# Five head pairs with some copies on other engines: ScalarE for VectorE, GpSimd for ScalarE

## The chip, the cores and the metric

The kernel runs on one core of a Trainium2 chip. A core has a matrix engine (TensorE, PE in the profile; its weight loads are PEld), and VectorE (DVE), ScalarE (ACT), GpSimd (POOL) and SyncE (SP), each with its own instruction queue, worked off in order. They meet through semaphores. SBUF is the on-chip memory, PSUM the eight banks that TensorE writes into; GpSimd works on SBUF here. The metric is the device time of one execution in microseconds: 692.33 us for the kernel before, the median of 3 runs (691.79 to 692.9). Lower is better.

## The reference

Attention with a threshold, for 8 batches of 8 heads, 576 positions, 64 columns per head, followed by a mixer:

```python
scores = scale * np.matmul(q, k.transpose(0, 1, 3, 2))
thresh = np.max(scores, axis=-1, keepdims=True) - tau
scores = np.where(scores >= thresh, scores, -1000000000.0)
scores = scores - np.max(scores, axis=-1, keepdims=True)
attn = np.exp(scores)
attn = attn / (np.sum(attn, axis=-1, keepdims=True) + 1e-09)
x = attn @ v                     # heads side by side: 576 x 512 per batch
h = x.transpose(0, 2, 1) @ U @ V # rank 32, along the positions
u = x + h.transpose(0, 2, 1)
out = u + np.maximum(u @ w_ch1, 0.0) @ w_ch2   # 512 -> 2048 -> 512
```

Inputs and output are float32. q, k and the scores are float32 in the kernel too; the weights of the attention, the turned u and the mixer are bf16, and v is split into two bf16 parts.

## The kernel before

**Tiling.** Two heads of a batch make a pair; there are 32 pairs, four to a batch. The 576 rows of a head are cut into four tiles of 128 and one of 64; the half tiles of two neighbouring pairs are put together, so an even pair has five row tiles (0 to 4) and an odd pair four (0 to 3). A row tile of two heads is a score step; there are 144 steps and 288 score tiles of 128 x 576.

**A step.** TensorE computes the scores (line 696) into one of two groups of three PSUM banks (`trio`). VectorE scales them into SBUF (`s_sb`) and keeps each row's least value `m` (line 725). GpSimd makes the threshold `thr` from `m` (line 742), a 128 x 2 instruction. ScalarE takes the exponential into `e_sb` (line 748). VectorE selects: it compares `s_sb` with `thr`, multiplies with `e_sb`, and sums each row (line 755), into `w_ring`. GpSimd doubles the last 64 columns (the twin copy, line 766), so that five blocks of 128 can be turned by TensorE into a PSUM bank (line 773). The turned weights are then copied from that bank into SBUF, `wT_ring` or `wT4`, by one 128 x 640 bf16 copy (line 781): head 0's by ScalarE, head 1's by VectorE, as the tuple `COPIED` says.

**The end of a pair.** TensorE multiplies the turned weights with the two parts of v (AV, lines 835 to 843). In the first four pairs ScalarE then takes the product to `x` (line 870) and GpSimd divides it by the row sums (line 874); later pairs do this through lines 890, 894 and 901. `narrow` makes a bf16 copy of x, `xb`, with two instructions on ScalarE (lines 906 and 907). TensorE applies U (914), ScalarE takes the result over as `tt` (920), TensorE applies V (929), VectorE adds it to x (936), which makes u. `narrow_u` makes the bf16 copy of u, `ub`, on ScalarE (943). TensorE turns it (951), ScalarE copies it out as `uT` (959).

**The mixer.** When the four pairs of a batch are done, its first product runs on TensorE in 16 pieces (line 1024, with 1040 for the half tile), ScalarE applies the ReLU (1014), and the second product (1057) gives the output tiles. These matmuls are spread among the score steps of later batches. W1 and W2 are loaded by GpSimd's queue in 8 pieces each (1127, 1130); q and k of the first pairs are loaded by SyncE, and of later pairs by GpSimd (563). v is loaded by SyncE (587).

**The order.** All work is written as tasks with an engine, a cost and what they depend on. A search, made beforehand, put the tasks in one order with those costs; its result is in the file as a list of task numbers, `ORDER`, and a table of the PSUM bank of each task, `BANK`. Negative numbers in the list are filler matmuls (line 526), whose result nobody uses. The kernel emits the tasks in the list's order, so each engine's queue is the list restricted to that engine. The costs stand in the code but nothing in the running kernel reads them.

Of the kernel before, what the change touches and what calls it, by code (L numbers as in the profile page):

```python
# [87 lines left out]
COPIED = (SCA, VEC)  # L88
PHASES = (1, 2, 3, 4, 5, 6, 8, 28)
# [4 lines left out]
HIGH = 32  # L94
# [20 lines left out]
class Task:  # L115
# [17 lines left out]
    24, 21, 26, 25, 19, 22, 23, 20, 1, 47, 0, 27, 45, 28, 44, 41, -1, -1, -1, -1, -1, -1, 32, 2, 34, 30, 46, 33, 35,  # L133
    31, 29, 48, -2, -2, 59, 43, 49, 61, 42, 60, 68, 39, -3, -3, -3, -3, -3, 73, 63, 62, 3, 69, 40, 74, 228, 70, 36,
    -8, -8, -8, 71, 75, 225, 77, 87, 64, 224, 56, 82, 72, 226, 89, 37, 227, -6, 52, 76, 88, 57, 50, 53, 231, 78,
    101, 4, 96, 83, 51, 90, 54, 102, 84, 55, 248, 65, 91, 38, 103, -8, -8, 85, 244, 115, 86, 110, 104, 92, 233, 79,
    105, 246, 117, 93, 58, 229, -3, -3, 94, 116, 80, 66, 249, 97, 81, 235, 130, 230, 67, 106, 95, 251, 111, 188,
    124, 247, 132, 112, 236, 118, 232, 98, 131, 107, 119, 245, -7, 108, 125, 189, 113, 99, 252, 109, 144, 120, 139,
    234, 100, 121, 250, 237, 126, 114, 5, 145, 122, 238, 191, 133, 146, 134, 140, 127, 153, 147, 239, 158, 128, 397,
    123, 141, 135, 192, 194, 240, 160, 148, 136, 142, 159, 241, 213, 149, 172, 214, 6, 195, 154, 167, 259, 150, 143,  # L140
    137, 161, 260, 257, 242, 174, 186, 138, 155, 243, 173, 258, -8, 156, 255, 162, 187, 157, 264, 175, 523, 181,
    168, 521, 256, 163, 169, 526, 266, 190, 151, 393, 265, 193, 152, 527, 196, 279, 7, 197, -7, -7, -7, -7, 207,
    402, 182, 164, 273, 524, 278, 267, 198, 176, 183, 396, 165, 274, 184, 166, 170, 129, 185, 275, 199, 280, 268,
    171, 399, -5, -5, 276, 177, 286, 291, 253, 269, 281, 178, 394, 277, 208, 8, 254, 282, 270, 179, 395, 205, 292,
    283, 200, 180, 525, 206, 293, 398, 210, 287, 300, 294, 400, 201, 288, 284, 392, 211, 261, 305, 289, 202, 271,
    306, 295, 262, 290, 272, 307, 296, 308, 318, 301, 313, 309, 285, 302, 319, 203, 297, 212, 405, 320, 204, 263,
    322, 333, 298, 406, 303, 209, 334, 407, 327, 375, 321, 314, 310, 299, 304, 315, 403, 341, 9, 328, 316, 376, 698,
    311, 215, 317, 408, 336, 335, 522, 323, -6, -6, 346, 404, 342, 332, 312, 337, 216, 699, 347, 373, 338, 694, 329,
    217, 324, 348, 343, 350, 401, 330, 360, 218, 349, 528, 344, 325, 361, 529, 363, 339, 378, 374, 695, 326, 362,
    331, 377, 345, 340, 520, 10, 364, 381, 355, 697, 412, 351, 368, 700, 356, 379, 696, 382, 380, 413, 530, 352,  # L150
    365, 414, 383, 693, -8, 531, 416, 409, 353, 426, 384, 369, 415, 354, -8, -8, 219, 535, 385, 427, 532, 370, 366,
    410, 421, 371, 220, 357, 533, 536, 417, 386, 447, 221, 367, 372, 418, 222, 422, 358, 534, 419, 223, 387, 359,
    423, 420, 11, 388, -5, 424, 429, 428, 425, 540, 439, 430, 389, 448, 440, 434, 431, 411, 541, 432, 542, 390, 719,
    441, 391, 554, 543, 544, 713, 555, 444, 449, 442, 545, 549, 567, 435, 433, 537, 445, 550, 562, 556, 569, 546,
    557, 12, 704, 568, 547, 446, 705, 706, 582, 551, 436, 570, 707, 581, 443, 437, 548, 708, 717, 438, 576, 558, -5,
    552, 715, 595, 709, 571, 563, 866, 450, 864, 577, 584, 13, 596, 451, 559, 553, 564, 452, 583, 589, 597, 871,
    565, 453, 560, 566, 720, 454, 561, 716, 458, 572, 455, 870, 604, 459, 598, -4, -4, -4, 456, 14, 651, 609, 457,
    599, 610, 464, 585, 622, 590, 612, 600, 465, 591, 623, 573, 460, 578, 611, 624, 538, 626, 601, 466, 539, 617,
    637, 461, 579, 636, 574, 714, 721, 467, 462, 605, 625, 575, 594, 580, 468, 868, 463, 618, 702, 733, 701, 469,
    627, 631, 723, 613, 652, 722, 632, 639, 703, 592, 734, 644, 633, 606, 586, 593, 619, 649, 15, 737, 470, 747,  # L160
    718, 735, 587, 471, 602, 638, 724, 628, 653, 588, 736, 748, 865, 607, 472, 725, 869, 608, 603, 640, 474, 749,
    473, 645, 614, 760, 475, 738, 671, 750, 739, 755, 761, 620, 742, 762, 615, 476, 616, 775, 763, 646, 764, 478,
    641, 774, 634, 743, 479, 642, 486, 477, 635, 744, 769, 621, 728, 726, 751, 643, 480, 1013, 756, 729, 487, 647,
    867, 481, 629, 770, 482, 1014, 630, 765, 776, 727, 659, 648, 483, 766, 484, 771, 672, 752, 777, 1015, 787, 485,
    16, 778, 660, 782, 1020, 661, 650, 757, 788, 1019, 655, 789, 779, 791, 1016, 740, 803, 790, 656, 745, 710, 741,
    681, 746, 753, 802, 682, 772, 662, 796, 780, 657, 673, 804, 781, 683, 654, 773, 754, 658, 792, 767, 877, 674,
    17, 768, 879, 758, 675, 711, 875, 880, 805, 759, 677, 783, 1186, 878, 676, 876, 797, 488, 678, 730, 810, 815,
    679, 663, 811, 1188, 842, 489, 684, 680, 816, 490, 18, 829, 712, 664, 817, 492, 665, 819, 1192, 830, 666, 491,
    493, 1018, 806, 685, 844, 831, 667, 832, 818, 812, 798, 784, 824, 494, 807, 731, 837, 793, 825, 686, 1017, 813,
    687, 794, 820, 1187, 668, 808, 785, 795, 826, 495, 814, 821, 809, 786, 833, 827, 845, 822, 496, 669, 838, 799,  # L170
    834, 670, 848, 843, 823, 839, 800, 732, 846, 835, 849, 828, 688, 836, 840, 850, 497, 1022, 841, -6, 884, 689,
    801, 1191, 690, 1021, 847, 872, 1189, 885, 1028, 874, 1024, 886, 1029, 1023, 1026, 1025, 898, 887, 873, 852,
    1212, 1027, 899, 691, 851, 921, 853, 888, 854, 855, 922, 1033, 893, 889, 1190, 692, 1211, 923, 894, 1209, 1034,
    499, 900, 890, 881, 1047, 1037, 500, 906, 1035, 895, 882, 891, 911, 1048, 896, 1193, 892, 913, 897, 1036, 901,
    907, 1060, 856, 902, 908, 914, 1042, 915, 1213, 912, 1050, 1062, 903, 501, 1208, 1055, 1061, 916, 857, 1038,
    1206, 909, 858, 904, 502, 910, 1049, 905, 1039, 1210, 1043, 859, 1040, 883, 503, 860, 917, 1069, 1075, 861,
    1207, 506, 1194, 1074, 918, 1030, 1041, 1195, 862, 919, 1199, 1051, 863, 1197, 924, 1200, 1056, 507, 1052, 1064,
    1088, 1077, 1057, 1063, 1076, 1065, 1082, 920, 1198, 1090, 508, 1066, 925, 1031, 1089, 1032, 1201, 1103, 1053,
    1202, 509, 1054, 1102, 1044, 1216, 1091, 1045, 1083, 498, 926, 1058, 927, 1070, 1067, 510, 513, 1110, 1215,
    1059, 1071, 1084, 1046, 928, 1104, 1068, 1214, 514, 929, 1097, 1196, 1078, 1072, 1092, 1115, 1073, 1087, 930,  # L180
    1093, 1105, 1094, 1116, 504, 933, 515, 934, 1117, 516, 935, 1111, 1118, 1085, 517, 931, 936, 1086, 1079, 932,
    1359, 1129, 937, 1080, 1144, 1130, 1081, 1098, 1119, 1095, 1226, 1145, 1106, 1137, 1120, 1107, 1096, 1146, 1124,
    1131, 1227, 938, 518, 1132, 1228, 1217, 1099, 1112, 939, 1138, 1363, 1100, 1221, 1148, 1125, 1360, 1222, 1218,
    1121, 1133, 1229, 1113, 1149, 940, 1235, 1114, 1362, 1101, 1142, 1152, 1358, 1241, 941, 1219, 1230, 1139, 1143,
    1126, 1174, 1236, 1220, 1108, 970, 1240, 1175, 1153, 1248, 1150, 1242, 944, 1109, 1176, 1492, 1231, 971, 1361,
    942, 1154, 1243, 1249, 1237, 1253, 1164, 945, 1357, 1165, 943, 1151, 1232, 1254, 1134, 1127, 1255, 1257, 1122,
    946, 1267, 1256, 1123, 1147, 1128, 1135, 511, 947, 1233, 1268, 1140, 1136, 1238, 1141, 1203, 1234, 948, 1258,
    1262, 1280, 1244, 1364, 1275, 1239, 1155, 1270, 1245, 1263, 1250, 949, 1281, 1166, 1204, 1156, 1205, 1295, 1157,
    1282, 1167, 950, 1264, 1158, 1284, 1269, 1168, 1283, 1246, 1296, 1177, 951, 1159, 1251, 1247, 1271, 1170, 1252,
    1368, 1160, 1171, 1223, 972, 1172, 1161, 1285, 1308, 1488, 973, 1276, 1297, 1369, 1298, 1277, 1173, 1309, 1289,  # L190
# [233 lines left out]
def kernel(  # L424
# [374 lines left out]
    def value_tasks(p):  # L799
# [105 lines left out]
        def narrow(_):  # L905
            nc.scalar.copy(out=pr.xb[:, 0:4, :], in_=bt.x[:, :, pr.cols])
            nc.scalar.copy(out=pr.xb[bt.h4, 4, :], in_=bt.x4[bt.h4, pr.cols])
# [34 lines left out]
        def narrow_u(_):  # L942
            nc.scalar.copy(out=pr.ub, in_=bt.x[:, :, pr.cols])
# [274 lines left out]
```

## Time and profile before

| | us |
|---|---|
| median of 3 runs | 692.33 (691.79 to 692.9) |
| profiled execution, its own time | 691.71 |
| its span | 689.9 |
| TensorE busy | 652.5 |
| VectorE busy | 554.8 |
| ScalarE busy | 521.9 |
| GpSimd busy | 453.8 |

The groups that the text returns to, over the whole run: the select, 288 instructions with 242.0 us; the score copy, 288 with 205.7; the exponential, 288 with 217.6; the weight copy, 144 on ScalarE and 144 on VectorE.

How to read the profile: a window lists for each engine the microseconds in which it was busy and, in brackets, its instructions; then the clock that TensorE was granted, as a share of full speed, and the share of the DMA engines. A group line gives the line of the kernel, the engine, the operation, what is written and read, the shapes, the count, the busy time, the mean duration in ns, the idle time of the engine just before these instructions and who ended it. Buffer numbers are left out of the names. A timeline line begins with the start and the duration in us. Instructions of one engine can overlap a little, so from start to start is often less than a duration.

### The profile page before, as it was taken

Reading aid. Unit: us, or ns where it says so; the run is one execution under the profiler, and the core shown is the slowest. Engines: PE = TensorE matmul, PEld = TensorE weight load, DVE = VectorE, ACT = ScalarE, POOL = GpSimd, SP = SyncE. Lnnn points to the kernel's source line nnn. Section 1 sums busy time; section 2 is a strip of 40 time slices with the busy share of each in tenths; the row PEclk is TensorE's granted clock in tenths of the full one; section 3 lists DMA queues with packets and bytes.
Section 4 is the critical chain, followed back from the end, with each engine's and each line's share of the span. In section 5 each row is a group of like instructions: output and inputs, shape, how many; then the busy total and the mean of one; then the engine's idle time right before and its main releaser. Section 6 shows DMA issues by size and latency. Waiting matters only on the chain.

```text
span 689.9 us, 19776 instructions
## 1 busy us (share of the span) xinstructions
PE 652.5 (95%) x7537; PEld 425.6 (62%) x7619; DVE 554.8 (80%) x1469; ACT 521.9 (76%) x1001; POOL 453.8 (66%) x887
## 2 busy tenths in 40 slices
PE   7988899999998999999999999999999999999997
PEld 3655655666666656566667667665666667656543
DVE  5999899889999998997889898899886987772102
ACT  3778779878888968878778788688877886767440
POOL 6566576887688786867887887788567665444020
PEclk9999999999999999999999999999999999999999
DMA  8664252422103132131122213323021321110223
GB/s 146 118 122 90 43 107 66 78 77 66 34 24 94 34 89 59 43 97 41 56 65 60 68 44 97 79 62 86 22 59 41 94 55 24 30 32 2 47 46 77
DMA packets 49503, 44.41 MB, mean 64 GB/s; under 512 B 28672, under 2 KB 40528, under 8 KB 49408
## 3 DMA queue, kind: packets, MB, share of 16 engines
q1 hardware_dynamic: 36320, 23.58, 14.5%
q0 software_dynamic: 12128, 19.22, 12.4%
q8 instruction: 60, 0.98, 0.6%
q10 hardware_dynamic: 960, 0.34, 0.2%
q14 instruction: 35, 0.29, 0.1%
HBM read 37.90 MB, written 9.44 MB: 69 GB/s over the span
## 4 chain that ended last, share of the span: by engine, by line
PE 57%; DVE 16%; ACT 7%; POOL 7%; issue 7%; DMA 4%; SPq 2%; another core or an unknown queue 0%; POOLq 0%; DVEq 0%; ACTq 0%
PE trio L696 12%; DVE w_ring L755 8%; PE trio L1057 8%; PE trio L1024 7%; DVE s_sb L725 6%; PE bank L1057 5%; PE bank L1024 5%; PE trio L773 4%; PE bank L839 3%; PE trio L839 3%; PE bank L773 3%; ACT e_sb L748 3%; POOL qkraw L563 2%; DVE wT_ring L781 2%; POOL x L901 1%
## 5 line engine op out<-in xcount | busy, mean ns | idle before, releaser
L755 DVE SCALAR_TENSOR_TENSOR w_ring<-s_sb,thr,e_sb 128x576 bf16<-128x576 f32 x288 | 242.0, 863 | 17.9 <-POOL thr L742 5.0
L748 ACT ACTIVATE e_sb<-s_sb,m 128x576 bf16<-128x576 f32 x288 | 217.6, 778 | 36.8 <-DVE s_sb L725 27.7
L725 DVE TENSOR_SCALAR_CACHE_REDUCE s_sb<-trio 128x576 f32<-128x576 f32 x288 | 205.7, 750 | 22.5 <-PE trio L696 18.2
L696 PE MATMUL trio<-qkT 64*64 64x288 f32 (+2 forms) x2304 | 160.1, 409 | 3.5 <-DVE wT_ring L781 1.3
L766 POOL COPY w_ring<-w_ring 128x64 bf16<-128x64 bf16 x288 | 89.6, 328 | 84.4 <-DVE w_ring L755 74.9
L773 PEld LDWEIGHTS <-w_ring 128*128 128x128 bf16 x1440 | 91.6, 98 | 48.7 <-issue 15.8
L696 PEld LDWEIGHTS trio<-qkT 64*64 64x64 f32 x2304 | 83.4, 132 | 52.1 <-issue 6.4
L1057 PEld LDWEIGHTS <-R 128*128 128x128 bf16 x576 | 52.6, 98 | 52.9 <-issue 5.6
L773 PE MATMUL trio<-identb,w_ring 128*128 128x128 bf16 x855 | 71.2, 219 | 6.3 <-DVE s_sb L725 3.1
L901 POOL TENSOR_TENSOR x<-x,rec 128x256 f32<-128x256 f32 (+1 forms) x84 | 51.9, 621 | 37.7 <-DVE x L894 33.2
L1024 PEld LDWEIGHTS <-W1b 128*128 128x128 bf16 x512 | 45.6, 98 | 49.2 <-issue 5.8
L563 POOL DMA_DIRECT2D qkraw<-in_q_dram x101 | 67.4, 668 | 9.5 <-PE bank L625 5.5
L742 POOL TENSOR_SCALAR thr<-m 128x2 f32<-128x2 f32 x144 | 44.5, 309 | 43.0 <-DVE s_sb L725 33.6
L1057 PE MATMUL bank<-W2b,R 128*128 128x512 bf16 x268 | 68.3, 379 | 1.8 <-issue 0.5
L563 POOL DMA_DIRECT2D qkraw<-in_k_dram x101 | 67.4, 668 | 3.8 <-issue 2.1
L1057 PE MATMUL trio<-W2b,R 128*128 128x512 bf16 x271 | 68.3, 379 | 1.4 <-ACT R L1014 0.7
L1024 PE MATMUL trio<-uT,W1b 128*128 128x512 bf16 x246 | 62.1, 379 | 3.2 <-DVE s_sb L725 2.3
L1024 PE MATMUL bank<-uT,W1b 128*128 128x512 bf16 x223 | 61.1, 379 | 1.3
L1014 ACT ACTIVATE R<-trio 128x512 bf16<-128x512 f32 x74 | 43.6, 602 | 23.7 <-PE trio L1024 16.8
L839 PEld LDWEIGHTS <-wT_ring 128*128 128x128 bf16 x896 | 55.0, 98 | 7.6 <-issue 4.9
L660 POOL TENSOR_TENSOR vh<-vraw_ring,vh 64x128 bf16<-64x128 f32 (+1 forms) x64 | 54.5, 852 | 2.8
L773 PE MATMUL bank<-identb,w_ring 128*128 128x128 bf16 x585 | 51.1, 219 | 4.1 <-DVE x L936 1.3
(116 smaller groups left out, 1025.3 us busy)
## 6 DMA issues: line engine op xcount, KB each, us to landing
out_dram<-o SPq DMA_DIRECT2D x71, 128.0 KB, 2.4
vraw_ring<-in_v_dram SPq DMA_DIRECT2D x32, 160.0 KB, 3.4
vraw_ring<-in_v_dram SPq DMA_DIRECT2D x32, 128.0 KB, 3.2
qkraw<-in_k_dram POOLq DMA_DIRECT2D x51, 80.0 KB, 2.5
qkraw<-in_q_dram POOLq DMA_DIRECT2D x50, 80.0 KB, 2.7
qkraw<-in_q_dram POOLq DMA_DIRECT2D x51, 64.0 KB, 2.4
qkraw<-in_k_dram POOLq DMA_DIRECT2D x50, 64.0 KB, 2.4
W1b<-in_moe_w_ch_dram POOLq DMA_DIRECT2D x8, 256.0 KB, 4.5
```

The source lines that it names most:

```text
L563: queue.dma_start(pr.qkraw[part, to, j, :], src[:, j, of, :])
L660: nc.gpsimd.tensor_tensor(out=pr.vh[part, tiles_, :, h, :], in0=raw[part, tiles_], in1=pr.vh[part, tiles_, :, 0, :], op=ALU.subtract)
L696: mm = nc.tensor.matmul(cols[part, lo:hi], a.tT[hs, 0, rows], a.tT[hs, 1, lo:hi], start=True, stop=True)
L725: nc.vector.tensor_scalar(out=s_sb, in0=score_cols(slot, x), scalar1=-scale, scalar2=None, op0=ALU.mult, op1=ALU.min, accum_out=m[:, x:x + 1])
L748: nc.scalar.activation(out=e_sb, in_=s_sb, func=ACT.Exp, bias=m[:, x:x + 1], scale=-1.0)
L755: nc.vector.scalar_tensor_tensor(out=w_sb[:, 0:S], in0=s_sb, scalar=thr_[:, x:x + 1], in1=e_sb, op0=ALU.is_le, op1=ALU.mult, accum_out=pr. ...
L766: nc.gpsimd.tensor_copy(out=w_sb[:, x, S:640], in_=w_sb[:, x, 512:S])
L773: nc.tensor.transpose(ps[:, kt * P:(kt + 1) * P], w_sb[:, kt * P:(kt + 1) * P], identb)
L839: nc.tensor.matmul(av[:, 2 * a + j, :], w, pr.vh[:, kt, j, :, :], start=kt == 0, stop=False)
L901: nc.gpsimd.tensor_tensor(out=x, in0=x, in1=over_sum(part), op=ALU.mult)
L1024: nc.tensor.matmul(bank[t.got[0]], W1b[:, dt, ft * P:(ft + 1) * P], bt.uT[:, dt, :], start=(dt == 0), stop=(dt == 3))
L1057: nc.tensor.matmul(ch, R2[:, ft, lo:lo + P], W2b[:, ft, :], start=(ft == 0), stop=(ft == 15))
```

## The change

`FRONT = 5`: in the pairs 0 to 4 two things differ. First, where the row tile's number is even (0, 2, 4), the copy of head 1's turned weights is made by ScalarE too, so that in these tiles ScalarE makes both heads' copies; that is three copies in pairs 0, 2 and 4 and two in pairs 1 and 3. Second, `narrow` and `narrow_u` use GpSimd's copy in place of ScalarE's: three instructions for each of the five pairs. Three costs in the task list are written anew with it (V's cast on GpSimd 1.1 to 0.72, the weight copy on VectorE 0.42 to 0.404, and those of the moved casts). With these the order was searched anew: `ORDER` and `BANK` are replaced as a whole. The list has 32 fillers in place of 43.

```diff
+FRONT = 5
 ...
-        t = done["vhi", p] = add(*(POOL, 1.1, top) if p < HIGH else (SCA, 0.62, high),
+        t = done["vhi", p] = add(*(POOL, 0.72, top) if p < HIGH else (SCA, 0.62, high),
 ...
-            def copy_w(_, x=x, t=t, on=nc.vector.tensor_copy if COPIED[x] == VEC else nc.scalar.copy):
+            mover = SCA if p < FRONT and i % 2 == 0 else COPIED[x]
+
+            def copy_w(_, x=x, t=t, on=nc.vector.tensor_copy if mover == VEC else nc.scalar.copy):
 ...
-            t = add(COPIED[x], 0.42 if COPIED[x] == VEC else 0.575, copy_w, [t], frees=[t])
+            t = add(mover, 0.404 if mover == VEC else 0.575, copy_w, [t], frees=[t])
 ...
+        front = p < FRONT
+        copy = nc.gpsimd.tensor_copy if front else nc.scalar.copy
+
         def narrow(_):
-            nc.scalar.copy(out=pr.xb[:, 0:4, :], in_=bt.x[:, :, pr.cols])
-            nc.scalar.copy(out=pr.xb[bt.h4, 4, :], in_=bt.x4[bt.h4, pr.cols])
-
-        xb = done["xb", p] = add(SCA, 0.71, narrow, xs + [got("tt_", p - 2), got("xb", p - 1)])
+            copy(out=pr.xb[:, 0:4, :], in_=bt.x[:, :, pr.cols])
+            copy(out=pr.xb[bt.h4, 4, :], in_=bt.x4[bt.h4, pr.cols])
+
+        xb = done["xb", p] = add(*(POOL, 0.78) if front else (SCA, 0.71), narrow, xs + [got("tt_", p - 2), got("xb", p - 1)])
 ...
         def narrow_u(_):
-            nc.scalar.copy(out=pr.ub, in_=bt.x[:, :, pr.cols])
-
-        ub = done["ub", p] = add(SCA, 0.515, narrow_u, [u, got("uT_", p - 2), got("ub", p - 1)])
+            copy(out=pr.ub, in_=bt.x[:, :, pr.cols])
+
+        ub = done["ub", p] = add(*(POOL, 0.6) if front else (SCA, 0.515), narrow_u, [u, got("uT_", p - 2), got("ub", p - 1)])
 ...
 ORDER = (...)   # 3,879 task numbers and 32 fillers, replaced as a whole
 BANK = {...}    # the PSUM bank of each task, replaced as a whole
```

## The prediction

> **What bounds the kernel now.** I read the busy shares first, then the windows by stage, then the groups of one window, then the durations and starts on VectorE and ScalarE. TensorE is busy 95% of the span, so the whole run looks like TensorE's. The stages differ:
>
> ```profile
> span 689.9 us, 19776 instructions
> PE 652.5 (95%) x7537; PEld 425.6 (62%) x7619; DVE 554.8 (80%) x1469; ACT 521.9 (76%) x1001; POOL 453.8 (66%) x887
> ```
>
> ```profile
> core 0: us, PE busy (x) PEld busy (x) DVE busy (x) ACT busy (x) POOL busy (x), PEclk, DMA share, GB/s
> 18.00:123.00 105.00, 94.01 (x1349) 62.53 (x1347) 99.35 (x274) 84.65 (x161) 67.89 (x150) 1.00 0.48 92
> 123.00:250.00 127.00, 120.28 (x1508) 82.45 (x1523) 116.69 (x308) 104.95 (x203) 98.00 (x188) 1.00 0.24 61
> 250.00:600.00 350.00, 341.87 (x3980) 228.02 (x4025) 303.34 (x798) 281.16 (x544) 253.61 (x489) 1.00 0.22 59
> 600.00:690.00 90.00, 83.05 (x619) 45.97 (x628) 25.78 (x61) 43.58 (x85) 22.92 (x36) 1.00 0.18 39
> ```
>
> The columns are TensorE, its weight load, VectorE, ScalarE, GpSimd. In 18:123 VectorE works 99.35 of 105 us, TensorE 94.01. In 250:600 it is the other way about: TensorE 341.87 of 350, VectorE 303.34. So the front, in which the first head pairs run and no mixer matmul stands before 94 us, is VectorE's; the rest is TensorE's. Nothing after the front is tied to a fixed time: what the front saves is handed on.
>
> The groups of VectorE in that window show what a saved microsecond would be made of, and that it hardly waits:
>
> ```profile
> line engine op names shapes xcount | busy us, mean ns | idle before us <-releasers
> L755 DVE SCALAR_TENSOR_TENSOR w_ring<-s_sb,thr,e_sb 128x576 bf16<-128x576 f32 x58 | 46.0, 825 | 0.9 <-ACT e_sb L748 0.9
> L725 DVE TENSOR_SCALAR_CACHE_REDUCE s_sb<-trio 128x576 f32<-128x576 f32 x59 | 41.8, 749 | 1.0 <-PE trio L696 1.0
> L781 DVE COPY wT_ring<-trio 128x640 bf16<-128x640 bf16 x14 | 6.8, 485 | 1.7 <-ACT wT_ring L781 1.6
> L781 DVE COPY wT_ring<-bank 128x640 bf16<-128x640 bf16 x10 | 4.7, 479 | 0.0
> ```
>
> With two smaller groups that wait (line 936 1.4, line 810 0.6) all its idle time in 105 us is 5.6 us. The 27 weight copies there (these 24 and 3 into wT) are the change's matter.
>
> **The copies taken from VectorE.** In pairs 0 to 4 the copies of head 1 at row tiles 0, 2 and 4 change engine: three each in pairs 0, 2 and 4, two each in 1 and 3, 13 in all. A copy lasts 0.485 us, but its end overlaps the next instruction's start, so I price by starts:
>
> ```profile
> start us, us, engine line op out<-in xcount [idle before <-releaser]
> 86.57 0.48 DVE L781 COPY wT_ring<-trio 128x640 bf16<-128x640 bf16 x1
> 86.97 0.80 DVE L755 SCALAR_TENSOR_TENSOR w_ring<-s_sb,thr,e_sb 128x576 bf16<-128x576 f32 x1
> ```
>
> 86.97 - 86.57 = 0.40 us of queue. 13 x 0.40 = 5.2 us, on the path: 4 copies are gone before the 17th score tile, 7 before the 33rd, 12 before the 49th, all 13 before the 65th, at 122 us. Had VectorE idled as before, the front would end 5.2 us sooner. That is the upper bound from this part. The lower bound comes from the chain of waits within 18:123, where the lines 755, 725 and 781 on VectorE hold 22.2 + 14.9 + 3.8 = 41%: if only that share of a saving arrives, 2.1 us does. VectorE's queue being full 95% of the window speaks for the upper end; I take 70%, 3.7 us.
>
> **The same copies on ScalarE, and what leaves it.**
>
> ```profile
> start us, us, engine line op out<-in xcount [idle before <-releaser]
> 59.16 0.71 ACT L781 COPY wT_ring<-bank 128x640 bf16<-128x640 bf16 x1
> 59.74 0.65 ACT L906 CAST xb_ring<-x 128x512 bf16<-128x512 f32 x1
> 60.26 0.31 ACT L907 CAST xb_ring<-x 64x128 bf16<-64x128 f32 x1
> 60.46 0.31 ACT L807 ACTIVATE rec<-d_ring,eps_t 128x10 f32<-128x10 f32 x1
> ```
>
> By starts a weight copy takes 0.58 us there, the two casts of x 0.52 and 0.20; the cast of u has the big cast's shape, 0.52. So ScalarE gets 13 x 0.58 = 7.5 us and loses 5 x 1.24 = 6.2 us: +1.3 us over five pairs. But not evenly: before the 33rd exponential (64.9 us) 9 copies have come and only two pairs of x and one u have gone, 5.2 - 2.0 = +3.2 us. From 37 to 65 us ScalarE is busy 22.38 of 28 us, from 18 to 123 84.65 of 105. It has 20 us free and takes 1.3 to 3.2. I cost it at nothing; the cover is that idle time, and if the copies fall where it has none the bound is 3.2 us. Each moved copy also ends some 0.2 us later (0.692 for 0.485), which holds a PSUM bank and an AV product; the other weight copies of the same tile are on ScalarE already, and three other banks turn meanwhile. Zero, at most 13 x 0.2 = 2.7.
>
> **The casts on GpSimd.** No such cast is in the trace. Nearest is its cast of V, 128x640, median 0.720 us, so 128x512 is estimated at 0.58; the 64x128 one lies between the 128x64 copy (0.238) and the 32x64 cast (0.285): 0.3. Per pair 0.58 + 0.30 + 0.58 = 1.46, in all 7.3 us, against 0.62 + 0.30 + 0.62 on ScalarE, so the chain from x to the low-rank product is no longer. GpSimd is busy 67.89 of 105 us and sits 24.5 us waiting for VectorE's select before line 766 and 5.8 before line 742. These 30 us are the cover. It fails where a cast, itself waiting for VectorE's sum of u (line 936) or for the norm, stands ahead of a threshold (742) or twin copy (766): the select and the turn on TensorE wait for these. The issues of weights and of q and k stand in the same queue and move with it. The last W1 piece is issued at 64.6 us against a first use at 94.0, cover 29 us; the last W2 piece at 131.9 us, with the fourth quarter of the first output tile waiting for it. A later W2 costs TensorE nothing while it has mixer products of line 1024 to do. Zero taken for all these, at most 7.3 us.
>
> **A rule against it.** Selects and GpSimd get in each other's way:
>
> ```profile
> L755 DVE SCALAR_TENSOR_TENSOR w_ring<-s_sb,thr,e_sb x288: 756/814/1943, 11.8 to 621.1; 128x576 bf16<-128x576 f32 x144
> L766 POOL COPY w_ring<-w_ring x288: 227/238/1003, 12.7 to 622.0; 128x64 bf16<-128x64 bf16 x144
> ```
>
> (min/median/max ns.) A select stretches to 1.94 us, a 0.24 us copy to 1.00. The select's mean in the whole run is 863 (its row of the page), so 288 x (863 - 814) = 14 us are lost over some 660 GpSimd instructions that are no DMA issue: 0.02 us each, 15 more give 0.3 us. The bound is every cast holding a select for its whole length, the 7.3 us again. I take 0.3. The Trainium skill, GPSIMD Engine Reference, section Specifications, says that GpSimd's SBUF interface is shared with VectorE and that instructions with two SBUF inputs contend; the select reads two, and the stretch agrees. By that rule taken strictly each cast would meet a select with the 44% of the window that selects fill and hold it half its 0.49 us: an estimate of 15 x 0.44 x 0.25 = 1.6 us, and the sum 1.3 us worse than mine.
>
> **The order.** Every queue is rearranged. Counted along TensorE's list, the mixer matmuls that stand ahead of each score step are the same within a few from step 32 on, the turns and AV products too. 11 of 43 filler matmuls (0.38 us each) go, 9 of them in the front; they stood in TensorE's waits, so 0. SyncE's first loads are reshuffled: pair 1's q goes ahead of V. The trace has waits for q of 0.6 us at 16.8 and 2.5 us at 70.0, so this can give or take up to 2.5; 0 taken. The rest beyond 123 us has 6.7 + 8.1 + 7.0 us of TensorE idle; a new order may win or lose a part; one tenth, 2 us, either way is my guess, and 0 is taken.
>
> **Sum.** -3.7 + 0.3 = -3.4 us. The profiled execution took 691.71 us (span 689.9 and 1.8 around it), 0.6 below the runs' median of 692.33. 691.7 - 3.4 = 688.3; against the median 692.3 - 3.4 = 688.9. I forecast 688.9 us.
>
> **Rivals.**
> A. The whole 5.2 us arrives, and with fewer waits at line 936 and 781 (1.4 + 1.6 us) a little more: 692.3 - 6 = 686. For it: the full queue. Against: ScalarE is 81% full and TensorE 90% in the same window.
> B. ScalarE becomes the bound of the front: the 3.2 us ahead of the 33rd exponential meet a stretch where VectorE wants to be 2.8 us shorter (7 copies). Then that part of the saving is void and only what comes behind it, 6 x 0.40 = 2.4 us at 41 to 70%, is left less some waiting: 691.3. For it: ScalarE waits for VectorE only 7.3 us in the window at line 748, so not much slack is truly ahead of it. Against: its 20 us of idle.
> C. Slower: GpSimd's queue. The casts delay thresholds and twins by their full 7.3 us; VectorE stands for it. 692.3 - 5.2 + 7.3 = 694.4. It decides for slower once over 6.6 of the 7.3 us come through (5.2 + 1.4), or 4.8 if only 3.4 us of saving arrives. For it: each wait is in order, and selects already wait for thresholds 7 times (5.0 us) in the run. Against: 30 us of slack.
> D. The change does not shorten the front since TensorE's order, not VectorE, sets it: 692.
>
> **How the numbers follow.** Mine 0.50 (own range 686.5 to 690.8), A 0.12, B 0.13, C 0.18, D 0.07. A measurement tells about 0.2%, 1.4 us, from no change. Faster (below 690.9) is mine, A and a little of B: 0.65. Same takes most of B and D: 0.16. Slower is C and D's tail: 0.19. The range runs from A's 685.5 to C's 694.8.
>
> **What would show it.** VectorE's 64th score tile, line 725 at 122 us, comes 3 to 4 us sooner, and the window before it has under 8 us of VectorE idle. VectorE's weight copies fall from 144 to 131. ScalarE's busy time in the front rises by 1 to 2 us. The casts on GpSimd take 0.58 and 0.3 us. From 123 us to the end the length stays within 2 us. I am wrong if VectorE's waits for line 742 or 748 in the front grow by more than 3 us, or if the rest behind the front has grown by as much as the front lost.

## The result and the profile after

The changed kernel took 694.82 us (median of 12 runs, 692.97 to 698.0), the kernel before, measured beside it, 691.9 (12 runs, 690.75 to 692.9): a ratio of 1.0041 [1.0029, 1.0054], 0.4% slower where 0.5% faster was forecast. Lines of the page of the changed kernel; the line of shares is the chain of work that ended last:

```profile
span 692.5 us, 19765 instructions
PE 652.4 (94%) x7527; PEld 424.3 (61%) x7608; DVE 560.7 (81%) x1456; ACT 526.4 (76%) x999; POOL 474.8 (69%) x902
...
PE 52%; DVE 20%; POOL 13%; issue 9%; ACT 4%; DMA 1%; ACTq 0%; SPq 0%; DVEq 0%; POOLq 0%
...
L755 DVE SCALAR_TENSOR_TENSOR w_ring<-s_sb,thr,e_sb 128x576 bf16<-128x576 f32 x288 | 254.9, 904 | 23.4 <-POOL thr L742 10.3
```

The chain and the select of the kernel before:

```profile
PE 57%; DVE 16%; ACT 7%; POOL 7%; issue 7%; DMA 4%; SPq 2%; another core or an unknown queue 0%; POOLq 0%; DVEq 0%; ACTq 0%
L755 DVE SCALAR_TENSOR_TENSOR w_ring<-s_sb,thr,e_sb 128x576 bf16<-128x576 f32 x288 | 242.0, 863 | 17.9 <-POOL thr L742 5.0
```

VectorE has 13 instructions fewer, as intended (1469 to 1456), and yet 5.9 us more of busy time: its select takes 904 ns in place of 863, and waits 10.3 us for thresholds in place of 5.0. GpSimd has gained 21 us and holds 13% of the chain (7% before). The windows by stage:

```profile
core 0: us, PE busy (x) PEld busy (x) DVE busy (x) ACT busy (x) POOL busy (x), PEclk, DMA share, GB/s
18.00:123.00 105.00, 95.77 (x1387) 64.65 (x1391) 102.15 (x274) 90.43 (x166) 81.25 (x166) 1.00 0.48 89
123.00:250.00 127.00, 120.92 (x1469) 81.87 (x1484) 116.61 (x307) 102.64 (x199) 105.97 (x200) 1.00 0.28 70
250.00:600.00 350.00, 335.82 (x3906) 222.40 (x3951) 304.49 (x784) 278.93 (x533) 254.92 (x476) 1.00 0.21 56
600.00:690.00 90.00, 86.68 (x672) 48.85 (x680) 27.81 (x66) 46.59 (x91) 21.65 (x38) 1.00 0.19 43
```

The first window is fuller than before on every engine. TensorE makes 38 matmuls more in the same 105 us; on VectorE the added time is that of longer selects. In 250:600 TensorE, which bounds that stretch, does 6 us less (335.82 for 341.87). So the front became faster and the rest slower. The time at which the n-th score tile starts on VectorE (line 725) shows where, after less before; a minus is sooner:

| tile (its time before, us) | 32 (62) | 64 (122) | 144 (290) | 176 (365) | 184 (376) | 224 (465) | 287 (614) | end |
|---|---|---|---|---|---|---|---|---|
| after | -2.3 | -5.2 | -4.5 | -5.8 | -2.6 | +2.4 | +1.8 | +2.6 |

This is a rough clock between two orders, since they place the score tiles differently among the other work: at the 72nd tile the changed kernel is 16.2 us ahead, at the 216th 3.9 behind. A lead counts where it stays. Up to the 176th tile the gain of the front is there. Then 3.2 us go in eight tiles (365 to 376 us of before) and 5.0 us in the next forty (376 to 465 us). The question for the runs was what stands there, and whether the moves or the new order put it there.

### The profile page after: what moved, and what is told of

The parts are those of the page before. It is cut to its first block, busy times and chain, and to the rows that moved or that the text cites. A ratio compares the mean times of both kernels' runs of the same rounds, so it can differ in the third digit from the quotient of the medians.

```text
span 692.5 us, 19765 instructions
## 1 busy us (share of the span) xinstructions
PE 652.4 (94%) x7527; PEld 424.3 (61%) x7608; DVE 560.7 (81%) x1456; ACT 526.4 (76%) x999; POOL 474.8 (69%) x902
## 4 chain that ended last, share of the span: by engine, by line
PE 52%; DVE 20%; POOL 13%; issue 9%; ACT 4%; DMA 1%; ACTq 0%; SPq 0%; DVEq 0%; POOLq 0%
PE trio L696 10%; DVE w_ring L755 9%; DVE s_sb L725 7%; PE trio L1062 7%; PE bank L1062 7%; PE trio L1029 5%; PE bank L1029 5%; POOL qkraw L563 4%; PE trio L841 3%; PE trio L773 3%; POOL w_ring L766 3%; PE bank L773 3%; PE bank L841 2%; DVE wT_ring L783 2%; POOL thr L742 1%
## 5 line engine op out<-in xcount | busy, mean ns | idle before, releaser
L755 DVE SCALAR_TENSOR_TENSOR w_ring<-s_sb,thr,e_sb 128x576 bf16<-128x576 f32 x288 | 254.9, 904 | 23.4 <-POOL thr L742 10.3
L766 POOL COPY w_ring<-w_ring 128x64 bf16<-128x64 bf16 x288 | 97.0, 350 | 76.2 <-DVE w_ring L755 65.2
L1062 PE MATMUL bank<-W2b,R 128*128 128x512 bf16 x299 | 76.3, 379 | 1.6 <-issue 0.5
L903 POOL TENSOR_TENSOR x<-x,rec 128x256 f32<-128x256 f32 (+1 forms) x84 | 54.7, 655 | 22.9 <-DVE x L896 17.1
L773 PE MATMUL trio<-identb,w_ring 128*128 128x128 bf16 x745 | 64.5, 220 | 5.5 <-DVE s_sb L725 4.2
L742 POOL TENSOR_SCALAR thr<-m 128x2 f32<-128x2 f32 x144 | 47.4, 329 | 32.0 <-DVE s_sb L725 21.9
L1081 POOL TENSOR_TENSOR o<-o,x 128x512 f32<-128x512 f32 x31 | 40.9, 1322 | 38.3 <-ACT o L1078 38.0
L1029 PE MATMUL bank<-uT,W1b 128*128 128x512 bf16 x229 | 63.2, 379 | 3.3 <-DVE x L896 1.2
L773 PE MATMUL bank<-identb,w_ring 128*128 128x128 bf16 x695 | 60.5, 219 | 6.0 <-POOL w_ring L766 4.1
L1062 PE MATMUL trio<-W2b,R 128*128 128x512 bf16 x244 | 60.2, 379 | 2.3 <-ACT R L1019 1.4
L1019 ACT ACTIVATE R<-trio 128x512 bf16<-128x512 f32 x75 | 44.6, 607 | 22.5 <-PE trio L1029 10.3
```

The source lines that it names most:

```text
L742: nc.gpsimd.tensor_scalar(out=thr_, in0=m, scalar1=tau_f, scalar2=None, op0=ALU.add)
L755: nc.vector.scalar_tensor_tensor(out=w_sb[:, 0:S], in0=s_sb, scalar=thr_[:, x:x + 1], in1=e_sb, op0=ALU.is_le, op1=ALU.mult, accum_out=pr. ...
L766: nc.gpsimd.tensor_copy(out=w_sb[:, x, S:640], in_=w_sb[:, x, 512:S])
L773: nc.tensor.transpose(ps[:, kt * P:(kt + 1) * P], w_sb[:, kt * P:(kt + 1) * P], identb)
L903: nc.gpsimd.tensor_tensor(out=x, in0=x, in1=over_sum(part), op=ALU.mult)
L1029: nc.tensor.matmul(bank[t.got[0]], W1b[:, dt, ft * P:(ft + 1) * P], bt.uT[:, dt, :], start=(dt == 0), stop=(dt == 3))
```

## The experiments

Each kernel's time is a median. The kernel before, measured beside them, took 691.8 to 692.4 us; intervals of the ratios are 0.0016 to 0.0034 wide, so a difference of two kernels is good to 1 us, with the widest to 1.5. Both files number their 3,879 tasks alike, so a kernel can take its moves from one file and its order and banks from the other, or the new order up to some task and from there the remaining tasks in the old order.

**The moves against the order.** The first four kernels:

```diff
 # moves_old_order: the changed kernel
-ORDER, BANK of the changed kernel
+ORDER, BANK of the kernel before
 # new_order_no_moves: the kernel before
-ORDER, BANK of the kernel before
+ORDER, BANK of the changed kernel
 # new_front_old_rest: the changed kernel; new order to score tile 78 (150 us), then the old
 # old_front_new_rest: the kernel before; old order to score tile 78, then the new
```

> The 13 weight copies and 15 casts change engine, but the task order and the PSUM banks stay those of before. Theory 1 (the moves help in the front, the new order loses it behind): the old order with a shorter VectorE queue, 2 to 4 us under before, about 688 to 690 us. Theory 2 (the moves themselves do the harm, by holding selects or by ScalarE): no gain or slower, 692 to 695 us.

> The new task order and banks, with every copy and cast on the engine it had before. Theory 1: it loses behind the front as the changed kernel does and lacks the saving in the front, about 5 us over the changed kernel: 699 to 701 us. Theory 2: without the moves the harm is gone, 690 to 693 us.

> The moves and the new order up to the 78th score tile (about 150 us), then the old order and banks for all tasks that remain. Theory 1: the front's saving of 5 to 6 us is kept to the end, 686 to 687 us. Theory 2: as slow as the changed kernel, 693 to 695 us. Theory 3 (what the front saves is lost in any case, because a later stage has a limit of its own): as before, 691 to 693 us.

> No moves and the old order up to the 78th score tile, then the new order and banks. Theory 1: no saving and the loss of some 8 us behind the front, about 700 us. Theory 2 and theory 3: as before, 691 to 693 us.

| | us | ratio |
|---|---|---|
| moves_old_order | 697.37 | 1.0086 [1.0073, 1.0099] |
| new_order_no_moves | 696.75 | 1.0067 [1.0055, 1.0079] |
| new_front_old_rest | 691.85 | 0.9998 [0.9990, 1.0007] |
| old_front_new_rest | 696.06 | 1.0061 [1.0048, 1.0073] |

Only new_front_old_rest came where one of its theories had it. The order by itself costs 4.7 us (696.75 - 692.03), and it does so with the old front before it as well: old_front_new_rest is 1.8 us ahead at the 176th tile and 4.5 behind at the 224th. The loss is in the rest of the new order, and the moves aren't needed for it. But the moves in the old order cost 5.3 us too; that is all there by the 72nd tile (+5.3) and stays to the end (+5.5). new_front_old_rest comes out at nothing: 5.1 us ahead at tile 64, 1.9 at tile 144, and 0 at the end. The two later joins below, with the same front, are 4.7 and 5.5 ahead at tile 144, so the join at tile 78 lost some 3 us.

**Which move, and how far the new order is good.**

```diff
 # new_order_copies_only: the changed kernel, casts back on ScalarE
-        copy = nc.gpsimd.tensor_copy if front else nc.scalar.copy
+        copy = nc.scalar.copy
 # new_order_casts_only: the changed kernel, weight copies as before
-            mover = SCA if p < FRONT and i % 2 == 0 else COPIED[x]
+            mover = COPIED[x]
 # new_to_101_old_rest, new_to_130_old_rest: the changed kernel; new order to score
 # tile 101 (199 us) or 130 (254 us), then the old
```

> The new order with the 13 weight copies on ScalarE, but the casts of x and u left on ScalarE too. Theory 1 (the casts on GpSimd hold VectorE's selects for some 3.3 us in the front and so eat most of the 5.2 us): the selects of the front stretch by 3 us less than in the changed kernel, and the time is 1 to 3 us below its 694.8: 692 to 694 us. Theory 2 (ScalarE has no room for 7.5 us more): slower than the changed kernel, 695.5 to 698 us.

> The new order with the casts on GpSimd, but the 13 weight copies left on VectorE. Theory 1: all the holding of selects and none of the saving, some 3 us above the new order without moves (696.75): 699 to 700.5 us. Theory 2: ScalarE, 7.7 us of casts lighter, helps: 693 to 696 us.

> The changed kernel up to the 101st score tile (about 199 us), then the order and banks of before. Theory 1 (what the front saves is handed on, and the 3 us that the run cut at the 78th tile lost between 117 and 157 us were lost at that seam): 686.5 to 688.5 us. Theory 2 (a saving is lost later in any order): 691 to 693 us.

> The changed kernel up to the 130th score tile (about 254 us), then the order and banks of before. Theory 1: the new order has lost some 2 us between tiles 112 and 128, the rest is handed on: 687.5 to 689.5 us. Theory 2: 691 to 693 us.

Measured: copies alone 694.63 (1.0028 [1.0012, 1.0044]), casts alone 699.11 (1.0103 [1.0089, 1.0117]); cut at 101 689.96 (0.9963 [0.9951, 0.9974]), cut at 130 689.04 (0.9956 [0.9943, 0.9970]). So in the new order:

| new order | no copies moved | copies moved |
|---|---|---|
| casts on ScalarE | 696.75 | 694.63 |
| casts on GpSimd | 699.11 | 694.82 |

Both moves together are worth -1.9 us there, the order +4.7, which makes the +2.8 that the change showed. And the same front with the old rest (new_to_130_old_rest) is 3 us faster than the kernel before: the start of the tiles is 5.5 us ahead at tile 144, 4.4 at 176, and 3.5 from tile 216 to the end, with no lasting change in the last 240 us. So the old rest hands on most of what the front saves, but not all: the 2 us between tiles 160 and 216 also go with the join at 101 (4.7 to 2.7) and with the one at 78 (1.9 to nothing), and no run says why.

**The block in the queues.** The changed kernel loses the first 3.2 us, between tiles 176 and 184, behind this. These lines are the timelines of SyncE, GpSimd, TensorE and VectorE of the changed kernel; the bracket is the idle time ahead and the releaser that the profile infers:

```profile
340.95 20.03 SPq L587 DMA_DIRECT2D vraw_ring<-in_v_dram  x2
361.09 0.54 SPq L795 DMA_DIRECT2D d_ring<-d_ring  x1
361.69 1.90 SPq L587 DMA_DIRECT2D vraw_ring<-in_v_dram  x3
...
359.15 1.16 POOL L660 TENSOR_TENSOR vh<-vraw_ring,vh 128x512 bf16<-128x512 f32 x1
...
361.16 0.33 POOL L742 TENSOR_SCALAR thr<-m 128x2 f32<-128x2 f32 x1
365.75 0.72 POOL L667 CAST vh<-vraw_ring 128x640 bf16<-128x640 f32 x1 [4.26 <-PE trio L1029]
366.55 0.43 POOL L660 TENSOR_TENSOR vh<-vraw_ring,vh 64x128 bf16<-64x128 f32 x1
367.07 0.60 POOL L742 TENSOR_SCALAR thr<-m 128x2 f32<-128x2 f32 x1
367.71 1.07 POOL L766 COPY w_ring<-w_ring 128x64 bf16<-128x64 bf16 x3
...
368.84 0.23 PE L773 MATMUL bank<-identb,w_ring 128*128 128x128 bf16 x1 [2.26 <-POOL w_ring L766]
...
371.56 0.76 DVE L725 TENSOR_SCALAR_CACHE_REDUCE s_sb<-trio 128x576 f32<-128x576 f32 x1 [3.22 <-PE trio L696]
```

In the new order SyncE issues the three loads of v of a pair not pair by pair: of pair 19 comes the second, then the first of pair 20, then the row sums' DMA (795), then the last of pair 19. The load of pair 20 needs a buffer that GpSimd frees with line 660, at 360.31 us (359.15 + 1.16). SyncE stands for it, and the last load of pair 19 stands behind it and is issued at 361.69, though it needs nothing that the second one did not need (the three loads of a pair wait for the same buffer). GpSimd's cast of v (667) waits for that load, and behind it in GpSimd's queue stand a threshold and three twin copies. TensorE's turn waits for the twins, VectorE's score copy for TensorE. The releaser named at the cast is a mixer matmul and can't be the real one; the load that was issued at 361.69 landed at 365.64 us by the trace, and the cast starts 0.1 us later. In the kernel before GpSimd's longest wait ahead of this cast is 1.0 us:

```profile
368.72 0.72 POOL L667 CAST vh<-vraw_ring 128x640 bf16<-128x640 f32 x1 [1.00 <-PE trio L696]
```

Two kernels put the loads of v in order, all of them in the first (24 of 96 move, each to behind the last load of the earlier pair), this one alone in the second; and the order of all of them was tried in the kernel before (33 move):

```diff
 # v_loads_in_order, one_v_load_moved, before_v_in_order: SyncE's queue in ORDER
-    v 19 second, v 20 first, sums, v 19 third, ...
+    v 19 second, sums, v 19 third, v 20 first, ...
```

> The changed kernel with one thing put otherwise on SyncE's queue: 24 of the 96 loads of v, those that stand ahead of a load of an earlier pair, go behind that load. Nothing else in the order moves. Theory 1 (behind the front the new order loses time because SyncE stands at a v load whose buffer is not free, with an earlier pair's last load behind it, and GpSimd then stands at the cast of v with thresholds and twin copies behind it: 4.26 us before the cast at 365.7 us): GpSimd's waits of 4.3, 2.3, 2.1 and 2.0 us before line 667 go, and the time falls by 2 to 4 us, to 691 to 693 us. Theory 2 (it is lost by selects held by GpSimd in the new order): no change, 694 to 695.5 us.

> The changed kernel with one v load (V20.0, the first of head pair 20) issued by SyncE behind the last v load of pair 19 instead of between them. Theory 1, this one block (the SyncE wait of 20.03 us that ends at 360.3 us, GpSimd's wait of 4.26 us behind it) is what loses the late part of the front's gain: TensorE's 2.26 us and VectorE's 3.22 us go, so 691.5 to 693 us. Theory 2, what pair order gives (4.8 us with 24 loads moved) is spread over many places: 694 to 695 us.

> The kernel before with 33 of its loads of v moved behind those of an earlier pair. Theory 1 (it only mends an order in which GpSimd waited for them; before, the longest such wait was 1.0 us): 690.5 to 692.5 us. Theory 2 (it is a gain in any order): 687 to 689 us.

| | us | ratio |
|---|---|---|
| v_loads_in_order | 690.03 | 0.9967 [0.9955, 0.9979] |
| one_v_load_moved | 691.34 | 0.9994 [0.9985, 1.0002] |
| before_v_in_order | 693.19 | 1.0018 [1.0009, 1.0028] |

One DMA issued ten places later in the list is worth 3.5 us (694.82 - 691.34), of 4.8 that all of them give; both came a little faster than the better of their theories. SyncE and GpSimd with the one moved:

```profile
357.51 0.48 SPq L795 DMA_DIRECT2D d_ring<-d_ring  x1
358.04 3.35 SPq L587 DMA_DIRECT2D vraw_ring<-in_v_dram  x4
...
361.05 0.80 POOL L667 CAST vh<-vraw_ring 128x640 bf16<-128x640 f32 x1 [0.45 <-PE bank L837]
```

SyncE now waits for the row sums to 357.51, issues the last load of pair 19 at 358.04, and waits for the buffer of pair 20 only behind it. The cast runs 4.7 us sooner, and the gain at the 184th tile is 5.6 us in place of 2.6. It isn't a law that pair order is better: in the kernel before the same sorting costs about 1 us (1.0 by the medians, 1.3 by the ratio), which arises between tiles 176 and 184. Nor did all of GpSimd's waits for v go: of 4.3, 2.3, 2.1 and 2.0 us in the changed kernel the last two stay in v_loads_in_order (2.1 and 1.9), where I expected none.

**What the loads leave.** one_v_load_moved still loses 5 us between tiles 184 and 224. The select in that stretch (in the four it begins at 371 to 376 us and ends at 460 to 468), in the kernel before, the changed one, the one with the load moved, and best_splice below, one fence each:

```profile
L755 DVE SCALAR_TENSOR_TENSOR w_ring<-s_sb,thr,e_sb 128x576 bf16<-128x576 f32 x40 | 34.4, 875 | 1.9 <-ACT qkT L631 1.1 <-ACT e_sb L748 0.7
```

```profile
L755 DVE SCALAR_TENSOR_TENSOR w_ring<-s_sb,thr,e_sb 128x576 bf16<-128x576 f32 x41 | 38.4, 949 | 5.5 <-POOL thr L742 3.4 <-ACT R L1019 1.3 <-ACT e_sb L748 0.6
```

```profile
L755 DVE SCALAR_TENSOR_TENSOR w_ring<-s_sb,thr,e_sb 128x576 bf16<-128x576 f32 x41 | 38.5, 952 | 5.6 <-POOL thr L742 3.4 <-ACT R L1019 1.3 <-ACT e_sb L748 0.6
```

```profile
L755 DVE SCALAR_TENSOR_TENSOR w_ring<-s_sb,thr,e_sb 128x576 bf16<-128x576 f32 x40 | 34.1, 866 | 2.9 <-POOL w_ring L766 1.1 <-ACT qkT L631 1.1 <-ACT e_sb L748 0.7
```

With the new rest a select is 75 ns longer, 3.0 us over 41, and 3.4 us are waits for the threshold; with the old rest neither is there. Both point to GpSimd: in the new rest its instructions stand beside the selects and ahead of the thresholds. That the new rest loses these 5 us is shown by best_splice, which has the old rest and loses 0.6 there; that the selects and thresholds are the cause is read from the trace, and no run took them away by themselves.

**The moves in the orders that keep the gain.** Four kernels price the moves there, the fifth does it in the old order, and the last asks what GpSimd's idle time is worth:

```diff
 # copies_new130_old / no_moves_new130_old: as new_to_130_old_rest, casts on ScalarE / no moves
 # v_order_copies_only / v_order_no_moves: as v_loads_in_order, casts on ScalarE / no moves
 # copies_old_order: as moves_old_order, casts on ScalarE
 # v_order_casts_twice: as v_loads_in_order, and in pairs 0 to 4
+            for _n in range(2 if front else 1):
                 copy(...)   # each of the 15 casts on GpSimd is made twice
```

> The new order up to the 130th score tile and the old one behind it, with the 13 weight copies on ScalarE and the casts left on ScalarE too. Theory 1 (the casts on GpSimd give nothing): 0.5 to 1.5 us below the 689.0 of the same splice with both moves, 687.5 to 688.5 us. Theory 2 (ScalarE needs the relief): 689.5 to 691 us.

> The same splice with no move at all. Theory 1 (a part of the front's saving is the new order's own): 690 to 691.5 us, between the splice with both moves and before. Theory 2 (it is the moves'): 692 to 694 us.

> The changed kernel with its loads of v in pair order, and the casts of x and u back on ScalarE. Theory 1 (on GpSimd the casts cost by holding selects what they spare ScalarE): the same as with both moves or up to 1.5 us less, 688.5 to 690 us. Theory 2 (ScalarE needs the relief): 691 to 693 us.

> The new order with its loads of v in pair order, and no move. Theory 1 (the moves are worth some 2 us wherever the rest is in order): 691.5 to 692.5 us. Theory 2 (what the loads of v held back had eaten more of the front's saving, so that the moves are now worth their full 5 us): 694 to 695.5 us.

> The old order with only the 13 weight copies moved to ScalarE. Theory 1 (in the old order the casts do the harm, since GpSimd stands at them with thresholds and twin copies behind): 690 to 692.5 us. Theory 2 (ScalarE's queue, in which the copies now stand, is what costs 5.4 us there): 695 to 697.5 us.

> The changed kernel with its loads of v in pair order, and each of the 15 casts on GpSimd in the first five pairs made twice, 7.3 us more on GpSimd. Theory 1 (each cast holds selects by a fifth of a microsecond or so): VectorE's selects in the front stretch by 2 to 4 us more, and the time rises by 1.5 to 4 us, to 691.5 to 694 us. Theory 2 (GpSimd's 30 us of slack hide it): 689.5 to 691 us.

| order | no moves | copies only | both | casts twice |
|---|---|---|---|---|
| old | 692.0 (before) | 692.07 | 697.37 | |
| new | 696.75 | 694.63 | 694.82 | |
| new, loads of v by pair | 692.43 | 689.16 | 690.03 | 696.74 |
| new to tile 130, then old | 692.62 | 688.54 | 689.04 | |

The second column against the first: the moved copies are worth 2.1 to 4.1 us in the three orders with the new front, and nothing in the old one. The third against the second: the casts cost 0.2 to 0.9 us beside the moved copies there, hardly to be told from nothing here, and 5.3 in the old order.

The first column settles what the order itself costs: with its loads of v by pair it is as fast as the kernel before (692.43 against 692.22, ratio 1.0002 [0.9994, 1.0010]). So nearly all of its 4.7 us hangs on where the loads of v stand in SyncE's queue.

The casts made twice cost 6.7 us more, where 1.5 to 4 was expected by way of longer selects. The selects are not it: those of the first 80 take 0.9 us more in sum. VectorE's idle time from 18 us to the 64th tile is 6.2 us in place of 2.3, 2.5 of it waits for thresholds. GpSimd's idle time doesn't hide what the order has no room for.

**The best of it.** The last kernel takes the new order with the loads of v by pair up to the 176th tile, the moved copies, the casts on ScalarE, and then the old order:

> New order with v loads in pair order up to score tile 176 (about 357 us), weight copies moved to ScalarE, bf16 copies left on ScalarE, and from there the order and banks of before. Theory 1, the front's gain is handed on as a constant shift and the old rest keeps it: 684.5 to 687 us. Theory 2, the two savings do not add (the seam or the old rest takes one of them back): 688.5 to 690 us, as with pair order and the copies alone.

686.91 us, 0.9922 [0.9909, 0.9935], 0.8% faster than before and the fastest of all. The tiles are 6.2 us ahead at the 64th, 7.3 at the 144th, 5.8 at the 176th, where the orders are joined, and 5.2 from the 200th to the last: behind the join the old rest keeps all but 0.6 us.

## Why the prediction was wrong

**The front: sooner than said, and in part by luck.** The 64th score tile came 5.2 us sooner, where 3 to 4 was said. VectorE is busy 102.15 of the first window's 105 us and makes 13 weight copies fewer. Its groups in 18:123 of the changed kernel answer to those shown of before:

```profile
L755 DVE SCALAR_TENSOR_TENSOR w_ring<-s_sb,thr,e_sb 128x576 bf16<-128x576 f32 x60 | 51.5, 884 | 0.8 <-POOL thr L742 0.4
L725 DVE TENSOR_SCALAR_CACHE_REDUCE s_sb<-trio 128x576 f32<-128x576 f32 x62 | 44.0, 744 | 0.2
...
L783 DVE COPY wT_ring<-bank 128x640 bf16<-128x640 bf16 x9 | 4.3, 473 | 0.0
L783 DVE COPY wT_ring<-trio 128x640 bf16<-128x640 bf16 x6 | 2.9, 486 | 1.8 <-ACT wT_ring L783 1.2 <-PE trio L773 0.6
```

62 score copies in place of 59, and waits of 0.4 us for the threshold: rival C's wait in the front did not come; that its 694.4 us is near the result is luck. Rival B did not come either: in v_order_copies_only ScalarE takes the copies and keeps the casts, and that is no slower than with the casts moved (689.16 for 690.03). ScalarE's busy time from the start to the 64th tile rose by 0.9 us (91.3 to 92.2), where 1 to 2 was said. But new_order_no_moves is 3.3 us ahead at the 64th tile, new_order_copies_only 6.7, the changed kernel 5.2: the copies gave 3.4, the casts took 1.5, and the rest of the lead is the order's, to which the prediction gave nothing. The order's part did not become time where it was tried: the new order without moves up to tile 130, then the old (no_moves_new130_old), takes 692.62 us, no less than before. Rival D is ruled out in the new order, since the copies add 3.4 there; in the old order it holds, as they add nothing.

**-3.7 for the copies: about right, on its condition.** -2.1 and -4.3 in the new order, -3.3 with the loads by pair, -4.1 with the old rest from tile 130, and 0 in the old order. "Had VectorE idled as before" was the condition. In the changed kernel VectorE idles less than before: 2.3 us between 18 us and the 64th tile, for 5.6. In the old order with the copies moved it idles 8.4 us there, and the tile comes 0.3 us later: what its queue lost came back as waits.

**+0.3 for the casts on GpSimd: the sum near, its reason wrong.** Beside the moved copies they measured +0.2 in the new order, +0.9 with the loads by pair, +0.5 with the old rest from tile 130, and +5.3 in the old order; without the copies +2.4 in the new order. Two of three durations were close (0.61 and 0.62 for 0.58), the third not. Their lines in the changed kernel (min/median/max ns):

```profile
L911 POOL CAST xb_ring<-x x5: 601/609/622, 39.4 to 125.4; 128x512 bf16<-128x512 f32 x5
...
L912 POOL CAST xb_ring<-x x5: 292/817/827, 40.0 to 126.1; 64x128 bf16<-64x128 f32 x5
...
L948 POOL CAST ub<-x x5: 608/622/1128, 50.3 to 140.0; 128x512 bf16<-128x512 f32 x5
```

Together they are 10.2 us for the 7.3 forecast. And they meet selects: the first 80 selects are in sum 5.3 us over their undisturbed 0.811 each, for 3.4 without the casts (new_order_copies_only), so 1.9 where 0.3 was taken. The mean of 0.02 us per GpSimd instruction was the mistake: it spread the stretch over all GpSimd instructions, and beside most of them there is none (below). What gave the difference back, so that only 0.2 to 0.9 us is left at the end, no run shows. The Trainium skill, GPSIMD Engine Reference, section Specifications, names the contention with VectorE instructions of two SBUF inputs; the 1.6 us estimated from that rule in the prediction was nearer to the 1.9 than the row's mean was. The 7.3 us of queue that were costed at zero, with 30 us of idle time as the cover, are near zero only where the order has placed them: 697.37 and 696.74 us are what they cost where it hasn't.

**Both moves together: as forecast, or somewhat less.** -3.4 was the sum. It measured -1.9 in the new order, -2.4 with the loads by pair and -3.6 with the old rest from tile 130. The moves are not where the prediction failed. Slips in the working change little: 70% of 5.2 is 3.6, and the rivals A and C come to 686 and 694.4 where the range takes 685.5 and 694.8.

**"The order": the step that failed.** It was put at 0, with a guess of 2 us either way, and the prediction said that nothing after the front is tied to a fixed time, so that what the front saves is handed on. Most of it is, as new_to_130_old_rest and best_splice show; but by the old rest, and the change replaced the rest too. The prediction's own sign of being wrong came: from the 64th tile to the end the changed kernel takes 7.7 us more than before, where the front had gained 5.2. The new order by itself measured +4.7 us, and 4.3 of these go when its loads of v are put by pair (692.43). With the moves one_v_load_moved settles 3.5, as one DMA at the head of SyncE's queue; the other loads of v are 1.3 more (690.03). About 1 us is left to the 689.04 of the old rest from tile 130, and 2.2 from 689.16 to 686.91 with the casts on ScalarE; the selects and thresholds of 376 to 465 us stand there in the trace, and that cause stays argued. I had counted TensorE's and VectorE's lists and found them nearly alike. I had not walked SyncE's list behind the front for a load that waits in front of one that is needed.

## What to carry to other kernels

When an order is searched anew, the new order is a change of its own, and here it was the larger one (+4.7 us against -1.9 for the moves): cost it by walking every in-order queue, the DMA-issuing ones too, for an entry that must wait for a late buffer and stands ahead of one that is due; here one such entry made 3.5 of a gain of 5.2 us disappear. To find where a gain goes, take the start of the n-th tile in both traces: the tiles between which the lead shrinks, and stays smaller, are the place to look. A lead in tiles is not yet a gain in time: the new order's own 3.3 us at the 64th tile became none. And where both orders number the same tasks, join the part of the new one that gains to the part of the old that keeps it; here that gave 2.2 us over the mended new order (689.16 to 686.91), and 5 with the copies and the loads by pair together (692 to 686.9).

## What the runs showed of the hardware

Not every GpSimd instruction stretches a select. Its mean duration, by what GpSimd ran beside it (over 30 ns of overlap; two-input first, then casts), from the starts and durations in the traces; DMA issues are left out:

| selects beside | before | after |
|---|---|---|
| none of these | 106, 0.81 us | 81, 0.82 us |
| 128x64 copies and thresholds | 97, 0.81 us | 101, 0.82 us |
| casts to bf16 | 13, 0.94 us | 26, 1.01 us |
| two-input instructions (lines 660, 874, 901 and 1076 of before) | 72, 0.99 us | 80, 1.07 us |

Of the selects in the first row 41 before and 33 after stood beside a DMA issue alone; they took 0.81 and 0.82 us. Beside two-input instructions the median is only 0.87 and 0.92, so many are hardly held; and a select that lasts long meets more instructions for that reason, which makes the lower rows look somewhat worse than they are.

Over 0.811 the two-input row is 12.8 us before and 20.3 after. The order makes the difference: with the new order and no move (new_order_no_moves) it is 21.0, with the moves in the old order 14.5. The longest select of the changed kernel, VectorE's line, then GpSimd's:

```profile
245.01 2.95 DVE L755 SCALAR_TENSOR_TENSOR w_ring<-s_sb,thr,e_sb 128x576 bf16<-128x576 f32 x1 [0.68 <-ACT e_sb L748]
...
245.06 0.41 POOL L766 COPY w_ring<-w_ring 128x64 bf16<-128x64 bf16 x2
245.41 0.63 POOL L563 DMA_DIRECT2D qkraw<-in_k_dram  x1
246.05 1.28 POOL L1081 TENSOR_TENSOR o<-o,x 128x512 f32<-128x512 f32 x1
247.27 0.78 POOL L766 COPY w_ring<-w_ring 128x64 bf16<-128x64 bf16 x1
```

Its cause isn't clear: at the usual 0.81 us it would have ended at 245.82, before the two-input instruction began, while GpSimd issued a DMA.

GpSimd's instructions are longer beside selects too: the twin copy that follows takes 0.78 us for its usual 0.24, and in the changed kernel the 64x128 cast took 0.82 in the four cases where a select ran beside it and 0.29 in the one where none did. Not always, though: in v_order_casts_twice such a cast that began 0.05 us after a select took 0.29 all the same.
